# Loading q four tokens to a partition, and reading it with a stride in the matmuls

## The chip, the cores and the metric

The kernel runs on one core of one Trainium2 chip. The metric is the device time of one execution in microseconds (us), median of several runs. The engines of a core are named as the profile names them: PE is TensorE (matmul), PEld its weight loads, DVE VectorE, ACT ScalarE, POOL GpSimd, SP SyncE, which here issues transfers.

## What is computed

The reference is a retention layer (attention with a decay in place of the softmax), followed by a feed-forward layer with a squared ReLU:

```python
# q, k, v: [B=8, H=8, S=576, D=64] float32
scores = q @ k.T / sqrt(64)
gamma  = 1 - 2 ** (-5 - h)                       # one per head
Dmat   = where(i >= j, gamma ** (i - j), 0)      # causal decay
ret    = (scores * Dmat) @ v
x      = ret.transpose(0, 2, 1, 3).reshape(4608, 512)
h      = x @ w_in                                # [4608, 2048]
out    = maximum(h, 0) ** 2 @ w_out              # [4608, 512]
```

## The kernel before

The 4,608 tokens are cut into 36 units: 32 full units of 128 consecutive tokens of one batch element, and 4 tail units (the last 64 tokens of two batch elements). Two units make a group. The first 8 units are loaded in pairs, two tokens to a partition; the change leaves them alone. That leaves 24 full units, and it is these that it touches.

Each of them is loaded with a partition per token, in rows of one head (64 float32, 256 bytes), cast to fp16 by GpSimd, and transposed by a DMA:

```python
            def fn(name=name, src=src):
                x = ld.tile([P, H, D], FP32, name=f"{name}32", tag=f"{name}32")
                tile_of[name + "32", u] = x
                if kind == "full":
                    nc.sync.dma_start(out=x, in_=src[b, :, c * P:(c + 1) * P, :].rearrange("h p d -> p h d"))
# ... cut ...
        def sorted_cast(op, out_, in_):
            op(out=out_.rearrange("p (n b a d) -> p n b a d", n=2, b=2, a=2),
               in_=in_.rearrange("p (n a b) d -> p n b a d", n=2, a=2))
# ... cut ...
        def fq():
            sorted_cast(nc.gpsimd.tensor_copy, tile_of["kq", u][:, 1], tile_of["q32", u])
# ... cut ...
        def fx2():
            t = tile_of["kqT", u] = work.tile([P, 2 * NP, P], FP16, name="kqT", tag="kqT", bufs=6)
            nc.sync.dma_start_transpose(out=t, in_=tile_of["kq", u].rearrange("p x n -> p (x n)"))
```

After the transpose, kqT holds for each pair of heads a block of 128 columns (tokens): the two heads of a pair lie in partitions 0 to 63 and 64 to 127. Blocks 0 to 3 are k, blocks 4 to 7 are q.

The retention is computed chunk by chunk of 64 tokens: scores inside a chunk, state times q for what went before. All these are small matmuls, 64 rows by 64 columns by 64, each in a quarter of TensorE's array, so that four run at once. They are written with `quad`, whose third operand is the one that streams through the array:

```python
    def quad(out_, lhsT, rhs, row, col, start=True):
        t = nc.tensor.matmul(out_, lhsT=lhsT, rhs=rhs, start=start, stop=True, skip_group_check=True,
                             tile_position=(64 * row, 64 * col))
# ... cut ...
    def emit_scores(g):
        tile_of["psc", g] = banks("psc")
        for s, u in enumerate(units_of(g)):
            kT = tile_of["kqT", u]
            ps = [x[:, cols(s)].rearrange("p (n i) -> p n i", i=64) for x in tile_of["psc", g]]
            for hp in range(NP):
                for a, c in ((0, 0), (1, 1), (0, 1), (1, 0)):
                    quad(ps[a][half(c), hp, :], kT[half(a), hp, half(c)], kT[half(a), NP + hp, half(c)], a, c)
# ... cut ...
    def inter(g, u, other):
        st = states(u)
        for n in range(2):
            for a, b in ((0, 0), (1, 1), (0, 1), (1, 0)):
                c = a ^ other
                if c in st:
                    x = 2 * n + b
                    put(g, u, c, 4 * n + 2 * a + b, tile_of[st[c][:2]][half(a), st[c][2], half(x)],
                        tile_of["kqT", u][half(a), NP + x, half(c)], a)
```

`states(u)` gives two states to a unit with an earlier chunk of 128 tokens in its batch element and one to the first such unit. The results go through VectorE (mask, decay) into xT, and from there into the feed-forward matmuls: `ph` (x times w_in) and `po` (times w_out; from the third group on in seven products instead of eight). In the profile, psc are the scores, psS the sums for the state (they read k and v only), psO the outputs of the retention, rT the masked scores.

A list scheduler in Python, run when the program is built, orders all these tasks; it has a duration for each, and the engines then run the orders that it made.

Of the kernel before, what the change touches and what calls it, by code (L numbers as in the profile page):

```python
# [103 lines left out]
def kernel(  # L104
# [9 lines left out]
    nc = tc.nc  # L114
# [78 lines left out]
        make_vdec(f"pair{e}", iota_pair[:, e:e + 1])  # L193


    heads = [(4 * n + 2 * a + b, n, a, b) for n in range(2) for a in range(2) for b in range(2)]
    lncol = const.tile([P, NP], FP32, name="lncol")
    lnrow_R = const.tile([P, NP], FP32, name="lnrow_R")
    for h, n, a, b in heads:
        nc.vector.memset(lncol[64 * b:64 * b + 64, 2 * n + a:2 * n + a + 1], lng[h])  # L200
        nc.vector.memset(lnrow_R[64 * a:64 * a + 64, 2 * n + b:2 * n + b + 1], lng[h])

    mask = const.tile([P, 64], FP32, name="mask")
# [79 lines left out]
    def add_load(u):  # L283
        kind, b, c = units[u]
        for n, (name, src) in enumerate((("k", k), ("q", q), ("v", v))):
            def fn(name=name, src=src):
                x = ld.tile([P, H, D], FP32, name=f"{name}32", tag=f"{name}32")
                tile_of[name + "32", u] = x
                if kind == "full":
                    nc.sync.dma_start(out=x, in_=src[b, :, c * P:(c + 1) * P, :].rearrange("h p d -> p h d"))  # L290
                else:
                    for i in range(2):
                        nc.sync.dma_start(out=x[i * 64:(i + 1) * 64],
                                          in_=src[b + i, :, 512:576, :].rearrange("h p d -> p h d"))
            loaded[name, u] = dma_task(0, 1.2 if loaded else 2.1, fn, acq=("ld",) if n == 0 else ())

    def add_load_pair(name, u):
        n = "kqv".index(name)
# [55 lines left out]
    def add_unit(u, base):  # L354

        kind, b, c = units[u]
        tail = [tail_dec] if kind == "tail" else []

        def sorted_cast(op, out_, in_):
            op(out=out_.rearrange("p (n b a d) -> p n b a d", n=2, b=2, a=2),  # L360
               in_=in_.rearrange("p (n a b) d -> p n b a d", n=2, a=2))

        def fk():
            t = tile_of["kq", u] = cast.tile([P, 2, H * D], FP16, name="kq16", tag="kq16")
            sorted_cast(nc.gpsimd.tensor_copy, t[:, 0], tile_of["k32", u])

        def fq():
            sorted_cast(nc.gpsimd.tensor_copy, tile_of["kq", u][:, 1], tile_of["q32", u])

        def fv():  # L370
            t = tile_of["v16", u] = cast.tile([P, H, D], FP16, name="v16", tag="v16")
            nc.gpsimd.tensor_tensor(  # L372
                out=t, in0=tile_of["v32", u],
                in1=vdec[kind].rearrange("p (h o) -> p h o", o=1).to_broadcast([P, H, D]), op=ALU.mult)
        ck = add("POOL", base, 0.65, fk, deps=[loaded["k", u]], acq=("kq",))
        cq = add("POOL", base + 1, 0.62, fq, deps=[loaded["q", u], ck])
        cv = add("POOL", base + 2, 1.1, fv, deps=[loaded["v", u]] + tail, acq=("v16",))
        for what, t in (("k", ck), ("v", cv)):
            for w in gate.get((what, u), []):
                sched.need(w, t)  # L380
        T["casts", u] = [ck, cq, cv]
        sched.free("ld", [ck, cq, cv])
# [3 lines that stand above are left out]
        T["kqT", u] = [add("SP", -1, 2.7, fx2, deps=[ck, cq], acq=("kqT",), after=3.0, lag=LAG_T)]  # L386

    def add_unit_pair(u, base):
# [4 lines left out]
        for i, name in enumerate("kqv"):  # L393
            xs[name] = []
            for e in range(2):
                eng = ("DVE" if (e if name == "v" else lead) else "ACT" if name == "k" and u >= 4 or u == 2 and e else
                       "DVE" if name == "q" and u == 2 else "POOL")

                def fc(name=name, e=e, eng=eng):
                    if (name + "x", u) not in tile_of:  # L400
                        tile_of[name + "x", u] = cast.tile([P, 2, H * D], FP16, name=name + "x", tag="kq16")
                    t = tile_of[name + "x", u][:, e]
                    x = tile_of[name + "32", u][:, :, e * D:(e + 1) * D]
                    if name == "v":
                        (nc.vector if eng == "DVE" else nc.gpsimd).tensor_tensor(
                            out=t.rearrange("p (h d) -> p h d", d=D), in0=x,
                            in1=vdec[f"pair{e}"].rearrange("p (h o) -> p h o", o=1).to_broadcast([P, H, D]), op=ALU.mult)
                    else:
                        engines[eng](out=t.rearrange("p (n b a d) -> p n b a d", n=2, b=2, a=2),
                                     in_=x.rearrange("p (n a b) d -> p n b a d", n=2, a=2))  # L410
                dur = (dict(POOL=1.1, DVE=0.6) if name == "v" else dict(POOL=0.62, DVE=0.4, ACT=0.59))[eng]
                xs[name].append(add(eng, base + (7 if name == "v" else i + e / 2), dur, fc, deps=[loaded[name, u]],
                                    acq=() if e else ("kq",)))
            if xs[name][0]["eng"] == xs[name][1]["eng"]:
                sched.need(xs[name][1], xs[name][0])
# [37 lines left out]
    def add_ret_pair(g):  # L453
# [29 lines left out]
        def fk():  # L483
            ps = rT["sum"] = banks("psS")
            for hp in range(NP):
                for e in range(2):
                    for s, a in ((0, 0), (1, 1), (0, 1), (1, 0)):
                        h = 4 * (hp // 2) + 2 * a + hp % 2
                        quad(ps[s][half(a), 64 * hp:64 * hp + 64], tile_of["kx", u][half(s), e, 128 * hp + 64 * a:128 * hp + 64 * a + 64],
                             tile_of["vx", u][half(s), e, 64 * h:64 * h + 64], s, a, start=hp == 0 and e == 0)  # L490
        t = add("PE", base + 4.5, 0.5, fk, deps=T["kvx", u], acq=("ff", "ff"))
# [29 lines left out]
        def inter(other):  # L521
            for n in range(2):
                for a, b in ((0, 0), (1, 1), (0, 1), (1, 0)):
                    s = a ^ other
                    if s or carry:
                        x = 2 * n + b
                        put2(s, 4 * n + 2 * a + b, before(s)[half(a), half(x)], kqT(s)[half(a), NP + x, :], a)

        def put2(s, h, lhsT, rhs, row):
            col = h % 2  # L530
# [4 lines left out]
        def fo1():  # L535

            tile_of["psO", g] = banks("psO")
            for m in range(NP):
                for e in range(2):
                    for s, b in ((0, 0), (1, 1), (0, 1), (1, 0)):  # L540
                        h = 2 * m + b
                        put2(s, h, tile_of["vx", u][half(s), e, 64 * h:64 * h + 64],
                             rT[e][half(s), m % 2, 2 * (m // 2) + b, :], s)

        def fo2():
            inter(0)
# [37 lines left out]
    def states(u):  # L584
# [4 lines left out]
        g, s = place_of[units[u]]  # L589
        return {1: ("Rm", g, s), 0: ("R", g - 1, s)} if c else {1: ("Rm", g, s)}  # L590

    def emit_scores(g):

        tile_of["psc", g] = banks("psc")
        for s, u in enumerate(units_of(g)):
            kT = tile_of["kqT", u]
            ps = [x[:, cols(s)].rearrange("p (n i) -> p n i", i=64) for x in tile_of["psc", g]]
            for hp in range(NP):
                for a, c in ((0, 0), (1, 1), (0, 1), (1, 0)):
                    quad(ps[a][half(c), hp, :], kT[half(a), hp, half(c)], kT[half(a), NP + hp, half(c)], a, c)  # L600

    def emit_sums(g):

# [3 lines left out]
        for s, u in enumerate(units_of(g)):  # L607
            if u not in full_of(g):
                continue
            ps = [x[:, cols(s)].rearrange("p (n i) -> p n i", i=64) for x in tile_of["psS", g]]  # L610
            for hp in range(NP):
                for c, a in ((0, 0), (1, 1), (0, 1), (1, 0)):
                    h = 4 * (hp // 2) + 2 * a + hp % 2
                    quad(ps[c][half(a), hp, :], tile_of["kq", u][half(c), 0, half(2 * hp + a)],
                         tile_of["v16", u][half(c), h, :], c, a)

# [11 lines left out]
# [4 lines that stand above are left out]
                c = a ^ other  # L632
                if c in st:
                    x = 2 * n + b
                    put(g, u, c, 4 * n + 2 * a + b, tile_of[st[c][:2]][half(a), st[c][2], half(x)],
                        tile_of["kqT", u][half(a), NP + x, half(c)], a)

    def emit_out1(g):
        tile_of["psO", g] = banks("psO")
# [3 lines left out]
    def emit_out2(g):  # L643
        for s, u in enumerate(units_of(g)):
            for m in range(NP):
                for c, b in ((0, 0), (1, 1), (0, 1), (1, 0)):
                    h = 2 * m + b
                    put(g, u, c, h, tile_of["v16", u][half(c), h, :],
                        tile_of["rT", g][half(c), s, m % 2, 2 * (m // 2) + b, :], c)
            inter(g, u, 0)  # L650

    QUAD = 0.0092
# [432 lines left out]
```

## Time and profile before

| | |
|---|---|
| time, median of 3 runs | 291.86 us (291.65 to 292.02) |
| span of the profiled execution | 289.7 us |
| PE busy | 281.1 us, 97% |
| ACT, DVE, POOL busy | 188.7, 181.2, 85.8 us |
| scores and other 64 by 64 matmuls | line L346 |
| load of q, full unit | 24 issues of 256 KB, 5.1 us to landing |
| cast of q by POOL | 28 of 661 ns |

Lines of the page: "L346" is line 346 of the kernel before. A group reads "out<-in, shapes, xcount, busy us, mean ns". In the 40 slices each digit is the busy share of a slice in tenths. A row of the chain or of the timeline begins with its start and its length in us. Matmuls overlap, so that the busy time of PE is not the time for which it streams; the distance from start to start is.

### The profile page before, as it was taken

Reading aid. Unit: us, or ns where it says so; the run is one execution under the profiler, and the core shown is the slowest. Engines: PE = TensorE matmul, PEld = TensorE weight load, DVE = VectorE, ACT = ScalarE, POOL = GpSimd, SP = SyncE. Lnnn points to the kernel's source line nnn. Section 1 sums busy time; section 2 is a strip of 40 time slices with the busy share of each in tenths; the row PEclk is TensorE's granted clock in tenths of the full one; section 3 lists DMA queues with packets and bytes.
Section 4 is the critical chain, followed back from the end, with each engine's and each line's share of the span. In section 5 each row is a group of like instructions: output and inputs, shape, how many; then the busy total and the mean of one; then the engine's idle time right before and its main releaser. Section 6 shows DMA issues by size and latency. Waiting matters only on the chain.

```text
span 289.7 us, 9992 instructions
## 1 busy us (share of the span) xinstructions
PE 281.1 (97%) x4322; PEld 233.3 (81%) x4322; DVE 181.2 (63%) x381; ACT 188.7 (65%) x361; POOL 85.8 (30%) x121
## 2 busy tenths in 40 slices
PE   7899999998999999999999999999999999999994
PEld 2568755787888888888888888888888888888883
DVE  3772369668585758736866757675777675455632
ACT  6459964684767676767767657586767676747830
POOL 5660035444434342342605151506240500000000
PEclk9999999999999999999999999999999999999998
DMA  7999999999899799999759699999994820201004
GB/s 197 276 208 205 249 289 256 183 228 210 186 185 211 158 225 198 214 223 231 149 147 211 139 226 198 180 190 211 226 179 140 186 83 2 75 2 72 2 6 141
DMA packets 139436, 49.94 MB, mean 172 GB/s; under 512 B 118144, under 2 KB 135040, under 8 KB 139392
## 3 DMA queue, kind: packets, MB, share of 16 engines
q1 hardware_dynamic: 134848, 44.84, 74.2%
q0 software_dynamic: 4224, 4.19, 8.8%
q8 instruction: 34, 0.56, 0.8%
q10 hardware_dynamic: 320, 0.26, 0.4%
q14 instruction: 10, 0.08, 0.1%
HBM read 36.70 MB, written 9.44 MB: 159 GB/s over the span
## 4 chain that ended last, share of the span: by engine, by line
PE 75%; DVE 1%; issue 0%; DVEq 0%
PE ph L853 36%; PE po L945 33%; PE psO L346 3%; PE psS L346 1%; PE psc L346 1%; DVE o L968 0%; DVE rT L673 0%; DVE p L997 0%; DVEq L968 0%
## 5 line engine op out<-in xcount | busy, mean ns | idle before, releaser
L853 PE MATMUL ph<-xT,w_in 128*128 128x256 f16 x1152 | 139.7, 273 | 0.1
L853 PEld LDWEIGHTS <-w_in 128*128 128x128 f16 x1152 | 110.9, 98 | 14.8 <-DMA w_in<-in_moe_w_in_dram 0.4
L861 ACT ACTIVATE rl<-ph 128x512 f16<-128x512 f32 x144 | 84.6, 588 | 49.6 <-PE ph L853 48.0
L871 ACT ACTIVATE gT<-rl 128x512 f16<-128x512 f16 x118 | 74.4, 631 | 3.4
L945 PEld LDWEIGHTS <-gS 128*128 128x128 f16 x512 | 49.5, 98 | 6.0
L945 PE MATMUL po<-wT,gS 128*128 128x256 f16 x384 | 51.9, 273 | 0.0
L922 DVE TENSOR_TENSOR gS<-gT,gS 128x512 f16<-128x512 f16 x64 | 32.5, 513 | 15.1 <-ACT gT L871 14.5
L945 PEld LDWEIGHTS <-gT 128*128 128x128 f16 x384 | 37.2, 98 | 5.3 <-issue 0.9
L922 DVE TENSOR_TENSOR gS<-gT 128x512 f16<-128x512 f16 x64 | 30.4, 477 | 15.7 <-ACT gT L871 15.6
L360 POOL CAST kq<-k 128x512 f16<-128x512 f32 x28 | 19.0, 679 | 63.8 <-DMA k<-in_k_dram 59.8
L945 PE MATMUL po<-w_out,gT 128*128 128x256 f16 x256 | 34.7, 273 | 0.7 <-DVE rT L673 0.7
L372 POOL TENSOR_TENSOR v<-v,vdec_full 128x512 f16<-128x512 f32 x24 | 26.6, 1107 | 20.2 <-DMA v<-in_v_dram 16.9
L360 POOL CAST kq<-q 128x512 f16<-128x512 f32 x28 | 18.5, 661 | 29.9 <-DMA q<-in_q_dram 29.7
L958 ACT COPY u<-po 128x256 f32<-128x256 f32 x32 | 11.8, 368 | 19.8 <-PE po L945 19.7
L968 DVE TENSOR_TENSOR o<-po,u 128x256 f32<-128x256 f32 x31 | 13.0, 420 | 16.0 <-PE po L945 9.3
L729 DVE TENSOR_TENSOR xT<-psO,gam_full 128x512 f16<-128x512 f32 x28 | 18.1, 685 | 6.5 <-PE psO L346 6.4
L873 DVE TENSOR_TENSOR gT<-rl 128x512 f16<-128x512 f16 x26 | 13.4, 517 | 12.4 <-ACT rl L861 11.9
L673 DVE TENSOR_TENSOR rT<-psc,mask 128x512 f16<-128x512 f32 x28 | 18.3, 683 | 3.4 <-PE psc L346 3.4
L968 DVE TENSOR_TENSOR o<-po,p 128x256 f32<-128x256 f32 x17 | 7.2, 423 | 16.7 <-ACT u L958 10.9
L945 PE MATMUL po<-w_out,gS 128*128 128x256 f16 x128 | 17.3, 273 | 0.0
L945 PE MATMUL po<-wT,gT 128*128 128x256 f16 x128 | 16.6, 273 | 0.0
L893 PE MATMUL po<-w_out,gT 128*128 128x512 f16 x64 | 15.8, 380 | 0.0
(78 smaller groups left out, 220.8 us busy)
## 6 DMA issues: line engine op xcount, KB each, us to landing
out_dram<-o SPq DMA_DIRECT2D x32, 256.0 KB, 3.5
k<-in_k_dram SPq DMA_DIRECT2D x24, 256.0 KB, 4.5
q<-in_q_dram SPq DMA_DIRECT2D x24, 256.0 KB, 5.1
v<-in_v_dram SPq DMA_DIRECT2D x24, 256.0 KB, 4.9
pair<-in_k_dram SPq DMA_DIRECT2D x4, 512.0 KB, 7.0
pair<-in_q_dram SPq DMA_DIRECT2D x4, 512.0 KB, 7.3
pair<-in_v_dram SPq DMA_DIRECT2D x4, 512.0 KB, 7.1
w_in<-in_moe_w_in_dram POOLq DMA_DIRECT2D x4, 512.0 KB, 8.9
```

Source lines behind the costliest of these rows:

```text
L346: t = nc.tensor.matmul(out_, lhsT=lhsT, rhs=rhs, start=start, stop=True, skip_group_check=True, tile_position=(64 * row, 64 * col))
L360: op(out=out_.rearrange("p (n b a d) -> p n b a d", n=2, b=2, a=2), in_=in_.rearrange("p (n a b) d -> p n b a d", n=2, a=2))
L372: nc.gpsimd.tensor_tensor(out=t, in0=tile_of["v32", u], in1=vdec[kind].rearrange("p (h o) -> p h o", o=1).to_broadcast([P, H, D]), op=ALU. ...
L673: tile_of["masking", g] = nc.vector.tensor_tensor(out=tile_of["rT", g][:, :, a], in0=tile_of["psc", g][a].rearrange("p (s n i) -> p s n i" ...
L729: nc.vector.tensor_tensor(out=tile_of["x", g].rearrange("p n (s c i) -> p c s n i", s=n, c=2)[:, c], in0=tile_of["psO", g][c].rearrange("p ...
L853: nc.tensor.matmul(tile_of["ph", g, fb][:, j, :], lhsT=w_in16[:, m, fi * P:(fi + 1) * P], rhs=tile_of["x", g][:, m, :], start=(m == 0), st ...
L861: nc.scalar.activation(out=t, in_=tile_of["ph", g, fb], func=ACTF.Relu)
L871: nc.scalar.activation(out=t, in_=rl, func=ACTF.Square)
L893: nc.tensor.matmul(tile_of["po", u], lhsT=tile_of["g", g][:, fi, s * P:(s + 1) * P], rhs=w_out16[:, fi, :], start=(fi == 0), stop=(fi == N ...
L922: nc.vector.tensor_tensor(out=Sx(k, h), in0=in0(h), in1=in1(h), op=op)
L945: nc.tensor.matmul(tile_of["pb", g, bank], lhsT=left(i), rhs=right[:, i, :], start=(start and i == 0), stop=(i == HF - 1), skip_group_chec ...
L968: nc.vector.tensor_tensor(out=o_tile(u)[:, half * HM:(half + 1) * HM], in0=bank(x), in1=tile_of[name, g], op=ALU.add)
```

## The change

For full units q is read from memory in rows of 1 KB: four consecutive tokens of a head are contiguous there. Partition 32j + r then holds tokens 4r to 4r+3 of heads j and 4+j. Each j is a transfer of its own, so that one load of q becomes four. Rows of 256 bytes make many packets; this is to make fewer of them.

The head pairs are renumbered to suit: a pair is now heads x and 4+x (before: 2 apart). GpSimd's cast of q puts the four tokens of a partition into four blocks. After the transpose, block t of q holds tokens 4r+t, for head pair x in columns 32x + r. Token order is thus a step of one block (128 fp16, 256 bytes) for three tokens out of four, and the matmuls read q in that order through a view with a stride. k, v, tails and pairs are loaded as before. The scheduler is told 1.8 us for the issue of such a q and 0.9 for k and v (before: 1.2 each).

```diff
-    heads = [(4 * n + 2 * a + b, n, a, b) for n in range(2) for a in range(2) for b in range(2)]
+    heads = [(4 * a + 2 * n + b, n, a, b) for n in range(2) for a in range(2) for b in range(2)]
...
-                if kind == "full":
+                if kind == "full" and name == "q":
+                    for j in range(NP):
+                        nc.sync.dma_start(out=x[32 * j:32 * j + 32].rearrange("r (a t) d -> r a (t d)", a=2),
+                                          in_=src[b, :, c * P:(c + 1) * P, :].rearrange("(a x) (r t) d -> x r a (t d)", a=2, t=4)[j])
+                elif kind == "full":
...
-            loaded[name, u] = dma_task(0, 1.2 if loaded else 2.1, fn, acq=("ld",) if n == 0 else ())
+            loaded[name, u] = dma_task(0, 1.8 if name == "q" and kind == "full" else 0.9 if kind == "full" else 1.2, fn, acq=("ld",) if n == 0 else ())
...
         def fq():
-            sorted_cast(nc.gpsimd.tensor_copy, tile_of["kq", u][:, 1], tile_of["q32", u])
+            if kind == "tail":
+                sorted_cast(nc.gpsimd.tensor_copy, tile_of["kq", u][:, 1], tile_of["q32", u])
+            else:
+                nc.gpsimd.tensor_copy(out=tile_of["kq", u][:, 1].rearrange("p (t a d) -> p a t d", t=4, a=2),
+                                      in_=tile_of["q32", u].rearrange("p (a t) d -> p a t d", a=2))
...
+    def qT(u, a, x, c):
+        t = tile_of["kqT", u][half(a), NP:]
+        if units[u][0] == "tail":
+            return t[:, x, half(c)]
+        return t[:, :, 32 * x + 16 * c:32 * x + 16 * c + 16].rearrange("p t r -> p r t")
...
-                    quad(ps[a][half(c), hp, :], kT[half(a), hp, half(c)], kT[half(a), NP + hp, half(c)], a, c)
+                    quad(ps[a][half(c), hp, :], tile_of["kqT", u][half(a), hp, half(c)], qT(u, a, hp, c), a, c)
...
-                    put(g, u, c, 4 * n + 2 * a + b, tile_of[st[c][:2]][half(a), st[c][2], half(x)],
-                        tile_of["kqT", u][half(a), NP + x, half(c)], a)
+                    put(g, u, c, 4 * a + x, tile_of[st[c][:2]][half(a), st[c][2], half(x)],
+                        qT(u, a, x, c), a)
```

The remaining lines of the diff renumber heads in the other casts, the decay tables, the sums and the output matmuls.

More of the change, by code (lines that the diff above doesn't have):

```diff
@@ L199 @@
     for h, n, a, b in heads:
-        nc.vector.memset(lncol[64 * b:64 * b + 64, 2 * n + a:2 * n + a + 1], lng[h])
+        nc.vector.memset(lncol[64 * b:64 * b + 64, h // 2:h // 2 + 1], lng[h])
         nc.vector.memset(lnrow_R[64 * a:64 * a + 64, 2 * n + b:2 * n + b + 1], lng[h])
@@ L360, in sorted_cast @@
             op(out=out_.rearrange("p (n b a d) -> p n b a d", n=2, b=2, a=2),
-               in_=in_.rearrange("p (n a b) d -> p n b a d", n=2, a=2))
+               in_=in_.rearrange("p (a n b) d -> p n b a d", n=2, a=2))
         def fk():
@@ L409, in fc @@
                         engines[eng](out=t.rearrange("p (n b a d) -> p n b a d", n=2, b=2, a=2),
-                                     in_=x.rearrange("p (n a b) d -> p n b a d", n=2, a=2))
+                                     in_=x.rearrange("p (a n b) d -> p n b a d", n=2, a=2))
                 dur = (dict(POOL=1.1, DVE=0.6) if name == "v" else dict(POOL=0.62, DVE=0.4, ACT=0.59))[eng]
@@ L487, in fk @@
                     for s, a in ((0, 0), (1, 1), (0, 1), (1, 0)):
-                        h = 4 * (hp // 2) + 2 * a + hp % 2
+                        h = 4 * a + hp
                         quad(ps[s][half(a), 64 * hp:64 * hp + 64], tile_of["kx", u][half(s), e, 128 * hp + 64 * a:128 * hp + 64 * a + 64],
@@ L526, in inter @@
                         x = 2 * n + b
-                        put2(s, 4 * n + 2 * a + b, before(s)[half(a), half(x)], kqT(s)[half(a), NP + x, :], a)
+                        put2(s, 4 * a + x, before(s)[half(a), half(x)], kqT(s)[half(a), NP + x, :], a)
         def put2(s, h, lhsT, rhs, row):
@@ L542, in fo1 @@
                         put2(s, h, tile_of["vx", u][half(s), e, 64 * h:64 * h + 64],
-                             rT[e][half(s), m % 2, 2 * (m // 2) + b, :], s)
+                             rT[e][half(s), m // 2, 2 * (m % 2) + b, :], s)
         def fo2():
@@ L595, in emit_scores @@
         for s, u in enumerate(units_of(g)):
-            kT = tile_of["kqT", u]
             ps = [x[:, cols(s)].rearrange("p (n i) -> p n i", i=64) for x in tile_of["psc", g]]
@@ L612, in emit_sums @@
                 for c, a in ((0, 0), (1, 1), (0, 1), (1, 0)):
-                    h = 4 * (hp // 2) + 2 * a + hp % 2
+                    h = 4 * a + hp
                     quad(ps[c][half(a), hp, :], tile_of["kq", u][half(c), 0, half(2 * hp + a)],
@@ L648, in emit_out2 @@
                     put(g, u, c, h, tile_of["v16", u][half(c), h, :],
-                        tile_of["rT", g][half(c), s, m % 2, 2 * (m // 2) + b, :], c)
+                        tile_of["rT", g][half(c), s, m // 2, 2 * (m % 2) + b, :], c)
             inter(g, u, 0)
```

## The prediction

> **What bounds the kernel now.** I read the page first, for the busy shares and the 40 slices:
>
> ```profile
> span 289.7 us, 9992 instructions
> ...
> PE 281.1 (97%) x4322; PEld 233.3 (81%) x4322; DVE 181.2 (63%) x381; ACT 188.7 (65%) x361; POOL 85.8 (30%) x121
> ...
> PE   7899999998999999999999999999999999999994
> ...
> DMA  7999999999899799999759699999994820201004
> ...
> q1 hardware_dynamic: 134848, 44.84, 74.2%
> ...
> q<-in_q_dram SPq DMA_DIRECT2D x24, 256.0 KB, 5.1
> ```
>
> Two things look full: TensorE to the end, the DMA engines until about slice 31 (225 us). Only one can set the pace, so I then read the chain that ended last in order of time. Here is one period of it, with the rows that the change touches (psc are the scores, psO the outputs):
>
> ```profile
> 130.22 0.87 PE ph L853 x8
> 131.10 0.25 PE psO L346 x16
> 131.34 0.26 PE psc L346 x32
> 131.60 2.29 PE ph L853 x20
> 133.89 0.38 PE psS L346 x32
> 134.27 0.40 PE psO L346 x48
> 134.67 0.98 PE ph L853 x8
> 135.65 0.44 PE po L945 x4
> ```
>
> One row begins where the last ends: TensorE runs from block to block without a hole. The 40 matmuls of 256 columns that the same chain shows from 86.69 us last 4.37 us, 109 ns each. Start times over the whole trace give the same: 109 or 110 ns for nearly every 256-column matmul after 70 us, while the DMA slices read 9. So the loads do not slow the matmuls. Then the waits of TensorE itself, in the first 80 us where loads are tightest:
>
> ```profile
> PE warm L250 <- DVE wT L163: 1.3, 1, 1.3
> PE po L945 <- DVE rT L673: 0.7, 1, 0.7
> ```
>
> The first is the start of the program. The second is the only stop that a load after 42 us (the first that the change can touch) could have had a hand in. Last, the DMA queue's own order of time, for how early q's data is there. Units 22 and 23 are transposed by
>
> ```profile
> 140.26 1.78 SPq L385 DMA_TRANSPOSE kqT<-kq  x1
> ...
> 147.19 1.30 SPq L385 DMA_TRANSPOSE kqT<-kq  x1
> ```
>
> and a transpose lands 4.3 us after issue (median of 28), so at 151.5 us; their scores begin at 159.19 us in the chain. That is 7.7 us of slack. For the very first unpaired group it is least: transpose issued at 54.34, landed near 58.6, scores at 61.88, 3.2 us.
>
> [...] a packet of 256 B took 22.0 ns on average (114,688 of them), one of 1 KB 65.9 ns, so 1 KB in four rows costs 88 ns and in one row 66. [...] no matmul of the kernel before reads with a stride[...].
>
> **The change part by part.**
>
> *Loads.* 24 full units beyond the eight paired ones load q in 1,024 rows of 256 B. Now 256 rows of 1 KB: 24 x 768 = 18,432 packets fewer, of 139,436. DMA time for one q: 1,024 x 22.0 / 16 engines = 1.41 us before, 256 x 65.9 / 16 = 1.05 after. That is 0.36 us per unit, 8.6 us over 24 units, about 5% of the engines' time between 45 and 230 us. It lies wholly beside a TensorE that does not wait for loads. What it can give back is at most the 0.7 to 0.9 us hole at 65 us; I count 0.3.
>
> *Issue.* One DMA per q becomes four, 72 more on SyncE's queue. An issue of a load takes at least 0.42 us in the trace, mostly about 1[...]. Four would be 4 x 0.43 = 1.7 us, where one took 0.6 to 3. So +0.7 us per unit at most, 1.4 us in a period of 14.6 us that two units share; the slack of 3 to 8 us takes that. Path: 0.
>
> *Cast.* GpSimd's cast of q writes four tokens by two halves instead of a sorted head order; runs of 64 elements on both sides as before, 661 ns as before. GpSimd is 30% busy. Path: 0. Renumbering of heads on the other casts, on the masks and on the decay tables changes only which block goes where. Path: 0.
>
> *Order.* The built program has the same number of TensorE and VectorE instructions; blocks of scores shift by a few matmuls (the first group's go behind 8 feed-forward matmuls, since the scheduler now thinks q later). No matmul is added. Path: +-0.3.
>
> *Strided reads.* This is the cost. q for one head and 64 tokens lay in 64 adjacent fp16 of kqT. Now tokens 4r to 4r+3 lie in four blocks of 128 columns, so consecutive columns are 256 bytes apart[...]. How many matmuls? Scores: 16 per unit x 24 = 384. State times q: 16 per unit with an earlier chunk (18 units) and 8 without (6 units): 288 + 48 = 336. Together 720, which run as 180 sets of four, each in its own quarter of the array. The chain gives 0.26 us for 32 scores, 8.1 ns each or 32.5 ns per set[...], so they cost 5.8 us now. [...] 180 x 26.7 = 4.8 us, all on the path, since TensorE is without holes. Sum in that case: 4.8 - 0.3 = +4.5 us, 296.4 us.
>
> **The rivals.**
>
> *The stride is free.* For: nothing in this trace shows a TensorE read limited by its pattern[...].[...] Then only the loads remain, -0.3 us or so: 291.5 us. As the DMA is off the path, not even this case brings a gain that matters.
>
> *Half rate.* 296.4 us as above.[...]
>
> *Worse than half.* Four matmuls run at once and two of each four read the same 64 partitions. [...] +80 ns x 180 = 14.4 us, 306 us.[...] Against: that the two streams collide is shown by nothing here.
>
> *The queue becomes the bound.* If each of the 96 small DMAs holds the queue as long as a large one does (1 us and more), two units take 8 us of a 14.6 us period for q alone; transposes and stores wait behind them and scores come late. Against: the slack[...]. It would cost 2 to 5 us and show as TensorE waiting for kqT.
>
> *DMA relief matters more than I think.* Against: the 109 ns, and the one hole. More than 2% (5.8 us) cannot come from it: all stops of TensorE after 42 us together, those at matmul-shape changes included, are about 10 us in the start times, and most are 0.1 us turns between blocks that stay.
>
> **Range and chances.** I give the free stride 45%, half rate 33%, worse 18%, queue trouble and the rest 4%. The middle of these lies between the two main cases; I name 294.0 us, knowing that the outcome is more likely near 291.5 or near 296.4 than at it. Range for 8 in 10: 290.8 to 304. The 2% line lies at 297.7, above the half-rate case with 1.3 us to spare: slower 0.24, same 0.74, faster 0.02.
>
> **What would show it.** Each step has its row. Stride: 32 scores in the chain, 0.26 us now; 0.26 again if free, about 0.47 at half rate, 0.9 if the streams share; the psO rows grow likewise by their strided part, while the psS rows, which read no q, must stay at 0.38. Loads: packets near 121,000, q still 256 KB per unit, now in 96 issues of 64 KB, and DMA slices a little lower between 45 and 230 us. Issue: SyncE's q rows near 1.7 us per unit and no TensorE wait for kqT. The 256-column pitch must stay at 109 ns. I am wrong if TensorE waits for a load or a transpose after 70 us, if the pitch moves, if the strided sets cost the same but the time still moves by over 1 us, or if the contiguous quarters slow down too.

## The result and the profile after

The changed kernel takes 305.33 us (median of 4 runs, 304.94 to 305.55), against 291.88 us of the kernel before in the same comparison: a ratio of 1.046, 95% interval 1.0442 to 1.0478. It is slower by 13.45 us, outside the range that was given, which ended at 304.

The page of the changed kernel, in the lines that answer to those shown of before:

```profile
span 303.7 us, 10112 instructions
...
PE 296.5 (98%) x4322; PEld 245.0 (81%) x4322; DVE 182.1 (60%) x381; ACT 189.2 (62%) x361; POOL 84.8 (28%) x121
...
PE   8999999999999999999999999999999999999994
...
DMA  7999999998979696999686799677896920101004
...
DMA packets 122156, 49.94 MB, mean 164 GB/s; under 512 B 94720, under 2 KB 117760, under 8 KB 122112
...
q1 hardware_dynamic: 117568, 44.84, 68.5%
...
q<-in_q_dram SPq DMA_DIRECT2D x96, 64.0 KB, 3.0
```

The loads did what they were made for: 17,280 packets fewer in all (18,432 fewer rows, as worked out, but 1,152 more packets of 4 bytes, 16 for each of the 72 further transfers), the share of the load queue down from 74.2% to 68.5% of a longer span. The count of TensorE's matmuls is the same, and its busy time has grown by 15.4 us, its weight loads by 11.7, while VectorE, ScalarE and GpSimd moved by 1 us or less.

Where TensorE's time went stands in the chain that ended last, in order of time. Each row is start, length, engine, line and number of instructions; line L350 holds the small matmuls (L346 before). This stretch of the changed kernel has blocks of full units and, between them, blocks of two tail units, which read q in adjacent columns as ever:

```profile
121.56 0.54 PE psO L350 x16
122.10 0.25 PE psc L350 x32
122.35 1.85 PE ph L867 x16
124.21 0.22 PE po L959 x2
124.42 0.81 PE psO L350 x48
...
136.04 0.25 PE psO L350 x16
136.29 0.88 PE psc L350 x32
137.18 2.29 PE ph L867 x20
139.47 0.38 PE psS L350 x32
139.84 0.40 PE psO L350 x48
```

Read it by pairs. The scores of the tails at 122.10 take 0.25 us, those of full units at 136.29 take 0.88, for 32 matmuls of one size in one kernel. The state blocks turn the same way: 16 at 121.56 (full units) take 0.54 us, 16 at 136.04 (tails) 0.25. The sums psS, which read no q, stay at 0.38 as before, and `ph` keeps its pace (16 in 1.85 us). Only what reads q with a stride has become slow: 0.88 us / 8 sets is 110 ns per set of four, where it was 32.5.

From start to start over the whole trace, the unpaired scores grew from 4.76 to 12.86 us, the two kinds of state matmuls from 6.33 to 12.29, the output matmuls that stand among them from 3.75 to 4.34: +14.7 us together (durations overlap and say less: a `ph` lasts 273 ns, and the next starts after 109). That is 1.2 us more than the time grew by, so the change saved about a microsecond elsewhere. The waits of TensorE show the larger part of it:

```profile
PE warm L250 <- DVE wT L163: 1.3, 1, 1.3
PE psS L350 <- POOL vx L413: 0.5, 1, 0.5
PE ph L867 <- DMA w_in<-in_moe_w_in_dram: 0.2, 1, 0.2
```

The wait of 0.7 us for rT at 65 us, which the kernel before had, is gone, and there is none for q, k or their transposes. So nothing here points to the queue of transfers, although it has more to do. This is the transfers' own order of time for one unit of the changed kernel:

```profile
128.80 0.58 SPq L294 DMA_DIRECT2D k<-in_k_dram  x1
129.42 2.41 SPq L291 DMA_DIRECT2D q<-in_q_dram  x4
131.88 0.43 SPq L294 DMA_DIRECT2D v<-in_v_dram  x1
```

Four issues of q last 2.4 us here and 1.9 to 3.8 elsewhere, rather than the 1.7 that I had worked out; v and k have become quicker to issue, in 0.43 and 0.58 us in the median (1.00 and 0.75 before).

### The profile page after: what moved, and what is told of

Read it like the earlier page. It is cut to its first block, busy times and chain, and to the rows that moved or that the text cites. A ratio compares the mean times of both kernels' runs of the same rounds, so it can differ in the third digit from the quotient of the medians.

```text
span 303.7 us, 10112 instructions
## 1 busy us (share of the span) xinstructions
PE 296.5 (98%) x4322; PEld 245.0 (81%) x4322; DVE 182.1 (60%) x381; ACT 189.2 (62%) x361; POOL 84.8 (28%) x121
## 3 DMA queue, kind: packets, MB, share of 16 engines
q1 hardware_dynamic: 117568, 44.84, 68.5%
## 4 chain that ended last, share of the span: by engine, by line
PE 92%; DMA 3%; issue 2%; POOL 2%; DVE 0%; POOLq 0%; DVEq 0%
PE ph L867 41%; PE po L959 32%; PE psO L350 7%; PE po L907 5%; PE psc L350 4%; DMA w_in<-in_moe_w_in_dram 3%; PE psS L350 2%; PE psT L432 1%; POOL mask L214 0%; POOL vx L413 0%; POOL w_in L324 0%; DVE o L982 0%; POOL mask L206 0%; DVE p L1011 0%; POOL mask L210 0%
## 5 line engine op out<-in xcount | busy, mean ns | idle before, releaser
L936 DVE TENSOR_TENSOR gS<-gT,gS 128x512 f16<-128x512 f16 x64 | 35.1, 554 | 12.8 <-ACT gT L885 12.2
L375 POOL CAST kq<-q 128x512 f16<-128x512 f32 x24 | 15.8, 657 | 32.0 <-DMA q<-in_q_dram 32.0
L887 DVE TENSOR_TENSOR gT<-rl 128x512 f16<-128x512 f16 x26 | 12.2, 470 | 12.6 <-ACT rl L875 12.3
L350 PE MATMUL psc<-kqT 64*64 64x64 f16 (+1 forms) x576 | 17.4, 259 | 0.1
```

Source lines behind the costliest of these rows:

```text
L375: nc.gpsimd.tensor_copy(out=tile_of["kq", u][:, 1].rearrange("p (t a d) -> p a t d", t=4, a=2), in_=tile_of["q32", u].rearrange("p (a t) d ...
L936: nc.vector.tensor_tensor(out=Sx(k, h), in0=in0(h), in1=in1(h), op=op)
```

## The experiments

Three theories stood open after this. *Loads*: the many small transfers and the shifted order cost it. *Sharing*: one strided stream runs at half rate, and two of them on the same partitions halve that again; this was the rival "worse than half" of the prediction. *Quarter*: each strided stream takes four times as long by itself, whoever else reads.

### The loads without the stride

```diff
-        return t[:, :, 32 * x + 16 * c:32 * x + 16 * c + 16].rearrange("p t r -> p r t")
+        return t[:, x, half(c)]
```

> The changed kernel with its new loads and casts of q, but the matmuls read 64 adjacent columns of q again (they read the wrong tokens, so what it computes is not the layer). Stride theory: the whole +13.4 us goes with the stride; 32 scores in the chain fall from 0.88 to 0.25 us, time 291.0 to 292.0 us, and no gain over before worth naming, since TensorE did not wait for loads. Load theory (the 96 small transfers and the later scores cost it): the time stays above 297 us.

Measured: 290.96 us, ratio to before 0.9964 (0.9952 to 0.9976). All of the loss is gone, and 1.0 us below the kernel before is left, which was not expected. The scores of the same block are back at their old length:

```profile
131.48 0.26 PE psc L350 x32
```

The theory of the loads falls.

### The stride without the loads

```diff
+    def qT(u, a, x, c):
+        t = tile_of["kqT", u][half(a), NP:]
+        if units[u][0] == "tail":
+            return t[:, x, half(c)]
+        return t[:, :, 32 * x + 16 * c:32 * x + 16 * c + 16].rearrange("p t r -> p r t")
...
-                    quad(ps[a][half(c), hp, :], kT[half(a), hp, half(c)], kT[half(a), NP + hp, half(c)], a, c)
+                    quad(ps[a][half(c), hp, :], kT[half(a), hp, half(c)], qT(u, a, hp, c), a, c)
...
-                        tile_of["kqT", u][half(a), NP + x, half(c)], a)
+                        qT(u, a, x, c), a)
```

> The kernel before, loads and casts as they were, only the matmuls of full units read q with the stride of the change (256 bytes, four blocks; wrong tokens, so what it computes is not the layer). Stride theory: 32 scores take 0.88 us and the time is 305 us within 1 us. Load theory: the time stays near 292 us.

Measured: 305.95 us, ratio 1.0478 (1.0457 to 1.0499). The stride by itself makes all of the loss: +14.0 us. (The chain counts 31 of the block's 32 scores.)

```profile
136.08 0.88 PE psc L346 x31
```

That is 0.6 us above the changed kernel, which has the small gain of the last run inside.

### One strided stream instead of two

```diff
-    def qT(u, a, x, c):
+    def qT(u, a, x, c, plain=False):
...
-        if units[u][0] == "tail":
+        if units[u][0] == "tail" or plain:
             return t[:, x, half(c)]
...
-                    quad(ps[a][half(c), hp, :], tile_of["kqT", u][half(a), hp, half(c)], qT(u, a, hp, c), a, c)
+                    quad(ps[a][half(c), hp, :], tile_of["kqT", u][half(a), hp, half(c)], qT(u, a, hp, c, plain=c == 1), a, c)
...
-                        qT(u, a, x, c), a)
+                        qT(u, a, x, c, plain=b == 1), a)
```

`plain` gives 64 adjacent columns. So of the two matmuls that run at once on the same 64 partitions (the four of a set start within about 10 ns in the traces of before and after), only one has a stride.

> The changed kernel, but of the two matmuls that read the same 64 partitions at the same time only one reads with the stride, the other reads adjacent columns (wrong tokens). Sharing theory (a strided stream alone runs at half rate, and the two streams on the same partitions halve that again): a set of four falls from 111 to some 57 ns, 32 scores from 0.88 to about 0.46 us, time about 296 us. Quarter theory (each strided stream by itself takes four times as long): the strided one of each pair still sets the pace, 32 scores stay above 0.8 us, time 303 to 305 us.

Measured: 305.61 us, ratio 1.0467 (1.0448 to 1.0487), a little above what the quarter theory had named. The chain of this kernel, the stretch of tails and full units again:

```profile
135.96 0.25 PE psO L350 x16
136.20 0.88 PE psc L350 x24
137.09 2.29 PE ph L867 x20
139.38 0.38 PE psS L350 x32
```

The block of scores takes 0.88 us as before, with half of the strided reads. (The chain counts 24 of its 32; some records fall outside it.) The start times in this block show the two kinds apart: from the second set on the strided matmuls follow each other at 110 to 112 ns, while the last adjacent one starts 0.33 us before the last strided one. A strided stream is as slow alone as beside another. Sharing falls, quarter stands.

### How slow at which step

Still open was what makes the read slow: any step, or a step of a certain size? One kernel reads with another step in each group, in the small score matmuls and in the feed-forward matmuls `ph`, which use the full array and one stream.

```diff
+    STEP = {9: 2, 10: 4, 11: 8, 12: 16}
+    ONE = {13: 16}
...
+        return kT[half(a)].rearrange("p x n -> p (x n)")[:, at:at + 63 * step + 1:step]
...
+    XSTEP = {9: 2, 10: 4, 11: 8, 12: 16, 13: 32}
...
+            return x.rearrange("p (i e) -> p e i", e=XSTEP[g])
+        if g == 14:
+            return x.rearrange("p (t r) -> p r t", t=4)
```

STEP is for the scores, XSTEP for `ph`; ONE gives the step to one of the two streams of scores.

> The kernel before, with the step between columns varied by group in two places (token order is wrong there, so what it computes is not the layer). (1) Feed-forward matmuls ph, full array, one stream of 256 columns, in groups 9 to 13 with steps of 2, 4, 8, 16, 32 fp16, in group 14 four blocks 64 columns apart read in turn: 109 ns each if free. [...] steps 2 and 4 (4 and 8 bytes) stay at 109 ns, from step 8 (16 bytes) on they are slow: 216 ns if a strided stream alone has half rate (sharing theory), 430 ns if a quarter (quarter theory). (2) Scores of groups 9 to 12 with steps of 2, 4, 8, 16 columns, two streams on the same partitions: 32 scores 0.26 us for steps 2 and 4, 0.88 us for 8 and 16. In group 13 only one of the two streams has step 16: 0.46 us for sharing, 0.88 us for quarter.

It took 401.7 us in one run. The chain has it in steps of 2, 4, 8 and 16 fp16 for the scores (32 matmuls a block; where a row counts fewer, some records fall outside the chain), and, in the rows of `ph` below, in steps of 2, 8, 16 and 32:

```profile
131.56 0.26 PE psc L346 x32
...
145.67 0.51 PE psc L346 x30
...
152.83 2.72 PE ph L875 x24
...
159.78 0.93 PE psc L346 x30
...
177.59 0.94 PE psc L346 x32
...
204.46 0.94 PE psc L346 x24
...
210.98 16.35 PE ph L875 x36
...
251.18 18.49 PE ph L875 x40
...
290.76 17.29 PE ph L875 x40
```

Scores: 0.26 us at a step of 4 bytes, 0.51 at 8, 0.93 at 16 and 0.94 at 32, and 0.94 with only one of the streams at 32. Median distances from start to start of `ph`, 256 columns:

| step, fp16 (bytes) | 1 (2) | 2 (4) | 4 (8) | 8 (16) | 16 (32) | 32 (64) | four blocks 128 bytes apart, in turn |
|---|---|---|---|---|---|---|---|
| ns | 109 | 113 | 227 | 451 | 460 | 430 | 435 |

Both expectations for step 4 were wrong: it is not free, it has half rate (227 ns, and 0.51 us for the scores). From 16 bytes on the cost stands still at a quarter (430 to 460 ns). The distance at a step of 8 is nearly the same at full and at about half of the granted clock (452 and 454 ns, see the end). Since the cost stops growing at a step of 16 bytes, I counted by 16 bytes, which hold eight fp16: step 2 uses four of them (113 ns), step 4 two (227), step 8 one (451).

### Elements in 16 bytes, or the step?

In the same figures the step and the number of used elements go together. Runs of adjacent elements, each run 32 bytes beyond the last, part them: the innermost step is always 2 bytes.

```diff
+    RUN = {9: 2, 10: 4, 11: 8}
+    WSTEP = {12: 2, 13: 4, 14: 8, 15: 16}
...
+            return x.rearrange("p (b h r) -> p h b r", r=RUN[g], h=16 // RUN[g])
...
+            return w_in16[:, m, at:at + 127 * WSTEP[g] + 1:WSTEP[g]]
```

> The kernel before with two things varied by group in the feed-forward matmuls ph (what they compute is not the layer). (1) Streaming operand in runs of 2, 4 and 8 adjacent fp16, each run 32 bytes beyond the last, groups 9, 10, 11. [...] runs of 4 and 8 stay at 109 to 115 ns, runs of 2 take about 225. Step theory (the innermost step decides, 2 bytes here): all three stay at 109. Jump theory (each jump costs): 2 slower than 4 slower than 8, all above 115. (2) Stationary operand (128 columns of w_in) with steps of 2, 4, 8, 16 fp16 in groups 12 to 15: if weight loads suffer as the stream does, the distance from matmul to matmul rises above 109 ns once a load takes over 109 ns, to 215 for steps 8 and 16; if not, 109 throughout.

One run, 300.02 us. `ph` in runs of 2 (first row), of 4 and of 8:

```profile
152.27 5.56 PE ph L868 x24
...
175.16 1.38 PE ph L868 x12
...
189.21 0.87 PE ph L868 x8
```

That is 232, 115 and 109 ns each. Half rate for two elements of 16 bytes (232 ns here, 227 at step 4), nearly full for four (115, and 113 at step 2), full for eight (109). The innermost step is the same in all three, so it is not what decides here; the number of elements used of 16 bytes goes with the pace in both kernels. In the stationary operand (the one of the weight loads) a step costs far less. The weight loads of groups 13 (step 4) and 14 (step 8), each from its own stretch; group 12 (step 2) has the usual 98 ns:

```profile
L868 PEld LDWEIGHTS <-w_in 128*128 128x128 f16 x62 | 6.6, 114 | 0.1
```

```profile
L868 PEld LDWEIGHTS <-w_in 128*128 128x128 f16 x64 | 7.1, 145 | 0.1
```

With step 16 it is 145 again, and the distance between the matmuls stays at 109 ns through all four groups. The time agrees: a group has 64 `ph`, and those at 232 and at 115 ns make 64 x 123 + 64 x 6 = 8.3 us more, where the run is 8.2 us above the kernel before (291.83).

### The new loads with reads in runs of 16

If four adjacent elements are nearly enough (115 ns for 109) and eight are (109), q may be read as it lies, 16 adjacent columns from each of the four blocks. The queries then stand in the order t, r; that needs a mask in this order and a reordering where VectorE makes xT, which reads the results of the matmuls from their memory, PSUM.

```diff
-        return t[:, :, 32 * x + 16 * c:32 * x + 16 * c + 16].rearrange("p t r -> p r t")
+        return t[:, :, 32 * x + 16 * c:32 * x + 16 * c + 16]
...
+        nc.vector.tensor_copy(out=mask_q.rearrange("p (t r) -> p t r", t=4), in_=mask.rearrange("p (r t) -> p t r", t=4))
...
+                        out=tile_of["x", g].rearrange("p n (s c r t) -> p c s n r t", s=n, c=2, t=4)[:, c],
+                        in0=tile_of["psO", g][c].rearrange("p (s n t r) -> p s n r t", s=n, n=NP, t=4),
```

> The whole layer, with the new loads of q, but the matmuls read q in the order in which it lies: for each of the four blocks 16 adjacent columns. The queries of a chunk then stand in the order t, r in scores and outputs; the mask of the scores is a copy in that order, and VectorE puts the tokens back in their order when it makes xT, reading PSUM with a step of 64 bytes in one operation per chunk. [...] 32 scores 0.26 us, time 290.8 to 291.8 us as with the loads alone, plus what the slower xT on VectorE (685 ns before, 28 of them) brings onto the path, at most 1 us. If any pattern of more than one piece is slow: above 297 us.

Measured: 291.09 us, ratio 0.9975 (0.9966 to 0.9984): the whole layer, some 14 us below the changed kernel and 0.7 below the kernel before. The scores in its chain, and VectorE's operation that makes xT for full units (duration in ns as min/median/max):

```profile
131.67 0.26 PE psc L351 x32
```

```profile
L753 DVE TENSOR_TENSOR xT<-psO,gam_full x24: 678/682/693, 70.1 to 248.4; 128x512 f16<-128x512 f32 x24
```

The reordering costs nothing: 682 ns, and 682 in the kernel before, although the reads from PSUM now step by 64 bytes.

### The other way to reorder

```diff
+                    for s in range(n):
+                        nc.vector.tensor_tensor(
+                            out=tile_of["x", g].rearrange("p n (s c r t) -> p s c n t r", s=n, c=2, t=4)[:, s, c],
+                            in0=tile_of["psO", g][c].rearrange("p (s n t r) -> p s n t r", s=n, n=NP, t=4)[:, s],
+                            in1=gam_f.rearrange("p n (c r t) -> p c n t r", c=2, t=4)[:, c], op=ALU.mult)
```

> The same, but xT is made in two operations of 256 elements per chunk instead of one of 512, which read PSUM contiguously, the decay table with a step of 16 bytes, and write xT with a step of 8 bytes. Twice as many operations, so xT comes 0.3 to 0.5 us later per group if their fixed cost counts; time 291 to 292.5 us. If reading PSUM with a step of 64 bytes is what is dear, this one is the faster of the two.

Measured: 294.41 us, ratio 1.0093 (1.0078 to 1.0108), above what was expected.

```profile
L754 DVE TENSOR_TENSOR xT<-psO,gam_full x48: 726/769/786, 70.3 to 252.2; 128x256 f16<-128x256 f32 x48
```

Half the elements take longer, 769 ns against 682, so a chunk takes 1.54 us instead of 0.68. The steps moved from the PSUM operand to the decay table in SBUF (16 bytes) and to the output (8 bytes); which of these two is dear was not parted.

### Where the last microsecond comes from

The loads alone left 1.0 us of gain. Is it the loads, or the order that the scheduler makes of the new durations?

```diff
-            loaded[name, u] = dma_task(0, 1.2 if loaded else 2.1, fn, acq=("ld",) if n == 0 else ())
+            loaded[name, u] = dma_task(0, 1.8 if name == "q" and kind == "full" else 0.9 if kind == "full" else 1.2, fn, acq=("ld",) if n == 0 else ())
```

> The kernel before, only the scheduler is told 1.8 us for q and 0.9 for k and v; loads, casts and reads are as before. Tells apart where the 1.0 us of the loads alone comes from. If it is the changed order (the scores of the first unpaired group behind 8 feed-forward matmuls, the 0.88 us hole at 65 us filled): 290.8 to 291.3 us. If it is the fewer packets: 291.7 to 292.2 us.

Measured: 291.01 us, ratio 0.9974 (0.9963 to 0.9985). It is the order. To see whether the loads add anything, both once more, side by side:

> The kernel before with the scheduler's new durations alone, again, beside the next one on the same chip. 291.0 us within 0.3.

> The changed kernel with adjacent reads (wrong tokens), again, beside the one above: new loads and new order. If rows of 1 KB bring nothing of their own, it stays within 0.3 us of the order alone; if the 18,432 fewer packets count, it is 0.5 us or more below.

Measured: the order alone 291.01 us, 0.9967 (0.9956 to 0.9979); loads and order 290.81 us, 0.9969 (0.9958 to 0.9980). No difference that these intervals can show. The chain of the kernel with the order alone:

```profile
60.93 1.09 PE po L945 x10
62.02 0.87 PE ph L853 x8
62.90 0.38 PE psc L346 x32
63.27 0.29 PE psS L346 x32
63.56 0.54 PE po L945 x4
```

In the kernel before, the scores stood ahead of the eight `ph` (this is its timeline, where a length runs to the end of the last matmul):

```profile
62.09 0.45 PE L346 MATMUL psc<-kqT 64*64 64x64 f16 x32
...
62.75 1.05 PE L853 MATMUL ph<-xT,w_in 128*128 128x256 f16 x8
...
65.83 1.03 PE L945 MATMUL po<-w_out,gT 128*128 128x256 f16 x8 [0.71 <-DVE rT L673]
```

Now they stand behind them, and the wait of TensorE for rT, 0.71 us in the last of these rows, is not among its waits any more. In the profiles TensorE's idle time between 60 and 80 us fell from 0.80 to 0.09 us. The times fell by 0.8, so about 0.1 is not placed, and why this order spares the wait was not followed further. The layer with the new loads and reads in runs of 16 (291.09 us) is no faster than this order alone either.

## Why the prediction was wrong

*What held.* TensorE's stream sets the time, and the loads lie beside it: removing packets gained nothing measurable (I counted 0.3 us), and 72 more issues cost nothing on the path (290.81 us with them, 291.01 with the order alone), though they last longer than worked out. The pitch of 256 columns stayed at 109 ns. The count of 720 strided matmuls in 180 sets was right, and the row to look at, 32 scores in the chain, showed the cost as named: "0.9 if the streams share".

*The step that failed* is the half rate: a set was to take 26.7 ns longer, 180 sets 4.8 us. That a read with a stride has half rate was my assumption, which no trace had shown, and 26.7 ns for the 64 columns of a set my estimate (the 109 ns of the trace for 256 columns give 27). The runs show a quarter: two elements of 16 bytes give half rate (227 and 232 ns for 109), and one, which is what the change reads, 430 to 460 ns. In place of 26.7 ns a set grew by 110 - 32.5 = 77.5 ns: 180 x 77.5 = 14.0 us instead of 4.8, which is what the stride alone cost (306.0 against 291.9). The free stride, to which I had given 45%, failed with it; the 294.0 us that I named lay between these two cases, and neither came. No matmul of the kernel before reads with a step, so nothing in its trace could tell them apart.

*The rival "worse than half"* came near in size (14.4 us) for a reason that fell: two streams on the same partitions did not hinder each other here. With one strided stream of the two on the same partitions a block of scores is as slow as with both (0.88 us), and a single stream on the full array has a quarter of its rate as well (430 to 460 ns for 109). So the size of that rival was luck: four times the estimate of 26.7 ns was right (110 measured), the reason was not. Because I tied the quarter to the sharing, and nothing showed sharing, I gave it 18% and let the range end 1.3 us too low.

*The order* was written down as +-0.3 us. It gave 0.8 to 1.0 us. I had named the move of the scores behind 8 `ph`, but had put the hole at 65 us down to the loads. With it the sum closes to 0.4 us: 14.0 - 0.9 = 13.1, measured 13.45.

## What to carry to other kernels

Before a streaming operand of a matmul is read with a stride, count the elements of each 16 bytes that are read in turn: here four fp16 were nearly enough (113 and 115 ns for 109), two gave half rate (227 and 232), and with one the matmul took four times as long (430 to 460). If a load with longer rows leaves data out of order, let the matmuls read runs as they lie and put the order right in an operation that is there anyway; here a VectorE operation out of PSUM did it for nothing (682 ns), while another way to write it took more than twice as long (1.54 us). And where no engine that sets the time waits for a load, fewer packets need not bring anything: here 17,280 fewer brought nothing that the intervals show. A small gain that comes with such a change may be the order of a scheduler, which one run with the durations alone shows.

## What the runs showed that I had not expected

- A step in the stationary operand was nearly free: the weight load grew from 98 to 145 ns at a step of 16 bytes and more, and the matmuls kept their 109 ns.
- VectorE read PSUM with an innermost step of 64 bytes as fast as without (682 ns for 512 elements with either).
- In the kernel with varied steps the granted TensorE clock (a share of full speed) was 1.00 in one stretch of slow `ph` and about half in another. The columns are the stretch, its length, PE's busy time, the clock, and the DMA share and rate:

```profile
200.00:210.00 10.00, 10.00 (x80) 1.00 0.33 45
210.00:220.00 10.00, 10.00 (x102) 0.63 1.25 240
220.00:230.00 10.00, 10.00 (x33) 0.52 0.19 32
...
240.00:250.00 10.00, 10.00 (x75) 0.50 0.00 1
```

The first three hold `ph` of group 11, step 8. These rows of the chain are 452 ns each at full clock and 454 at 0.63 and then 0.52:

```profile
199.93 3.62 PE ph L875 x8
...
210.98 16.35 PE ph L875 x36
```

Reads of adjacent columns did follow the clock; this row lies in the stretch at 0.50:

```profile
242.81 1.71 PE po L967 x8
```

That is 214 ns each, where they take 109 at full clock. The read at a step of 8 did not follow the granted clock; what sets its pace instead, and what lowered the clock, no run here shows.
